# Ten weight chunks leave PSUM before they are split, in a fused attention and feed-forward kernel

## The chip, the cores and the metric

The kernel runs on one core of a Trainium2 chip. The time is the device time of one execution in microseconds (us), taken as the median of several runs. The engines are TensorE (PE: matmuls, PEld its weight loads), VectorE (DVE), ScalarE (ACT), GpSimd (POOL) and SyncE (SP, which issues the DMAs here). SBUF is the on-chip memory, PSUM the small one into which TensorE writes.

## What is computed

Windowed attention, then a feed-forward layer with a rational activation, then a gated one. All is float32, over 2304 tokens:

```python
h = x @ w_in                       # x: attention output, 2304 x 512; w_in 512 x 2048
P = a[0] + a[1]*h + a[2]*h*h + a[3]*h*h*h
Q = 1.0 + abs(b[0])*abs(h) + abs(b[1])*h*h
x = (P / (Q + 1e-06)) @ w_out      # w_out 2048 x 512
gate = 1.0 / (1.0 + np.exp(-(x @ w_gate)))          # w_gate, w_val 512 x 1536
out = (gate * (x @ w_val)) @ w_out2
```

## The kernel before

A float32 operand is split into a high part, which TensorE's fast float32 form takes exactly, and a low part, the difference. A product is then three fast matmuls (`mm3`, L741): high by high, high by low, low by high. Tokens are cut into five blocks of up to 512. The phases are (1, block 0), (2, block 0), and then blocks in pairs; phase kind 1 is the rational layer (`step1`, L752), kind 2 the gated one (`step2`). A step treats one weight chunk of 128 features. In the first phase there are 16 steps: `hidden` (12 matmuls into a bank of pool "h"), the activation, and `product` (matmuls on L841, whole float32 in this phase alone).

The activation of a step is a chain over three engines: on ScalarE the cubic (L775), the abs (L771), the slope (L780), the logarithm (L798) and its exponential (L801), `rest` (L815); on GpSimd `quad` (L789) and `correct` (L820); on VectorE two `horner` (L792), `check` (L804) and `ratio` (L823). A step takes up to four temporaries of pool "t" (11 tiles in SBUF) for it; the one of the cubic is held until `product` has read it.

Weights come in float64, as pairs of 32-bit words, and `weights` (L406) makes float32 of each chunk at its first use: a load on SyncE (L420), `rescale` (L429), `sign` (L442, GpSimd), `shift` (L445, VectorE), `low_bits` (L450, VectorE), then `hi` (a copy, L320 on ScalarE, L322 on VectorE, L324 on GpSimd) and `lo` (a subtraction, L327 on VectorE or GpSimd). A store (L404) follows for chunks that are used again. The intermediate lies in a tile of pool "t" (`wt`) for the first eight chunks and for those of the second layer. For the other chunks of w_in and w_out in the first phase (`banked`) it lies in PSUM, in one of the two buffers of pool "a" (`wb`). GpSimd doesn't read PSUM in this kernel, so for `banked` chunks only ScalarE does `hi` and only VectorE does `lo`. Chunks of w_out are kept `whole` in the first phase and have neither.

Who does what, and in which order, is set by a list planner (`Plan`, L59) at build time. An operation has a priority (its due time), one or more ways (an engine and a cost each), and slots that it takes and uses. An operation that can go to several engines goes where its estimated end is best. A slot is free again when all that use it are planned to be done; an operation that can't get one of a pool holds back those behind it that take from the same pool. Ways marked PORT (VectorE instructions whose operands lie in SBUF, and all of GpSimd's) are planned one at a time over both engines; `dvep` marks a way without that. Each engine then runs its instructions in the planned order.

Of the kernel before, what the change touches and what calls it, by code (L numbers as in the profile page):

```python
# [7 lines left out]
F32 = mybir.dt.float32  # L8
F32R = mybir.dt.float32r
BF16 = mybir.dt.bfloat16  # L10
U32 = mybir.dt.uint32
# [49 lines left out]
class Plan:  # L61
# [14 lines left out]
    def op(self, prio, ways, fn, deps=(), takes=(), uses=(), after=None, table=None):  # L76


        o = Op(prio, ways, fn, deps, takes, uses, after, table)
        for s in o.uses:  # L80
            s.left += 1
        for d in o.deps:
            d.next.append(o)
        if after:
            after.then.append(o)
        self.ops.append(o)
        return o
# [133 lines left out]
def act(n, psum=False, ptrs=0):  # L221
    return ("ACT", n / 1200 + (0.05 if psum else 0.093) + 0.093 * ptrs)


def dve(n, ptrs=0):

    return ("DVE", n / 960 + 0.15 + 0.03 * ptrs, *PORT)


def dvep(n, ptrs=0):  # L230

    return ("DVE", n / 960 + 0.14 + 0.03 * ptrs)


def dve2(n, ptrs=0):
    return ("DVE", n / 1920 + 0.15 + 0.03 * ptrs, *PORT)


def pool(n):
    return ("POOL", n / 477 + 0.17, *PORT)  # L240


def pool1(n, ptrs=0):
    return ("POOL", n / 960 + 0.07 + 0.03 * ptrs, *PORT)


def dma(nbytes, count=1):
    return ("SP", nbytes / Plan.DMA_RATE, count)
# [3 lines left out]
def tile_window_attention__rational_ffn__glu(  # L252
# [48 lines left out]
    op = plan.op  # L301
# [7 lines left out]
    def tile_of(slot, shape, dt=F32, name=None):  # L309
        return pools[slot.pool].tile(shape, dt, tag=slot.pool, name=name or slot.pool)  # L310
# [4 lines left out]
    def temp(slot, name, dt=F32):  # L315
        return tile_of(slot, [P, 512], dt, name)

    def copy(e, out, in_):
        if e == "ACT":
            nc.scalar.copy(out, in_)  # L320
        elif e == "DVE":
            nc.vector.tensor_copy(out, in_)  # L322
        else:
            nc.gpsimd.tensor_scalar(out=out, in0=in_, scalar1=1.0, scalar2=1.0, op0=ALU.mult, op1=ALU.mult)  # L324

    def lo_part(e, out, in_, hi):
        ENGINES[e].tensor_tensor(out=out, in0=in_, in1=hi.bitcast(F32), op=ALU.subtract)  # L327
# [10 lines left out]
    lnb, two, exb = (biases[:, n:n + 1] for n in range(3))  # L338
# [59 lines left out]
    def place(z, keys):  # L398
        for key in keys:
            chunk[key] = z["hi"], z["lo"]  # L400

    def keep(c, what):
        d = stored[c] = dr.tile(list(what.shape), F32, tag=f"w{c[0]}{c[1]}", name=f"w{c[0]}{c[1]}")
        nc.sync.dma_start(out=d, in_=what)  # L404

    def weights(c, prio, keys, again):  # L406

        n = before.get("n", 0)
        before["n"] = n + 1
        banked = c[0] in "iO" and n >= 8
        whole = c[0] == "O"
        raw_s, t_s, w_s = Slot("w"), Slot("a" if banked else "t"), Slot("w")
        z = {}

        def load(e):
            z["w"] = tile_of(raw_s, [P, 1024], U32, "wraw")
            nc.sync.dma_start(out=z["w"], in_=srcs[c[0]][c[1]].bitcast(U32))  # L420
            z["low"], z["high"] = (z["w"].rearrange("p (f t) -> p f t", t=2)[:, :, n] for n in range(2))

        def rescale(e):
            t = z["t"] = tile_of(t_s, [P, 512], U32, "wb" if banked else "wt")
            w = z["c"] = tile_of(w_s, [P, 2, 512], F32R, "w")
            z["hi"], z["lo"] = w[:, 0, :], w[:, 1, :]
            x = z["high"].bitcast(F32)
            if e == "ACT":
                nc.scalar.activation(out=t.bitcast(F32), in_=x, func=AF.Copy, scale=REBIAS * REBIAS)  # L429
            else:  # L430
                ENGINES[e].tensor_scalar(
                    out=t.bitcast(F32), in0=x, scalar1=REBIAS, scalar2=REBIAS, op0=ALU.mult, op1=ALU.mult
                )

        def sign(e):
            if e == "DVE":
                nc.vector.tensor_scalar(
                    out=z["high"], in0=z["high"], scalar1=0x80000000, scalar2=None, op0=ALU.bitwise_and
                )
            else:  # L440
                x = z["high"].bitcast(F32)
                nc.gpsimd.tensor_scalar(out=x, in0=x, scalar1=0.0, scalar2=0.0, op0=ALU.mult, op1=ALU.mult)  # L442

        def shift(e):
            nc.vector.scalar_tensor_tensor(  # L445
                out=z["t"], in0=z["t"], scalar=3, in1=z["high"], op0=ALU.logical_shift_left, op1=ALU.bitwise_or
            )

        def low_bits(e):
            nc.vector.scalar_tensor_tensor(  # L450
                out=z["hi"].bitcast(U32) if whole else z["t"], in0=z["low"], scalar=29, in1=z["t"],
                op0=ALU.logical_shift_right, op1=ALU.bitwise_or,
            )
            if whole:
                for key in keys:
                    chunk[key] = z["hi"].bitcast(F32)

        def hi(e):
            copy(e, z["hi"], z["t"].bitcast(F32))

        def lo(e):
            lo_part(e, z["lo"], z["t"].bitcast(F32), z["hi"])
            place(z, keys)

        def store(e):
            keep(c, z["hi"].bitcast(F32) if whole else z["c"].bitcast(F32))

        o = before["load"] = op(
            -200.47 + 0.92 * n if n < 8 else prio - 6.66,
            [dma(4096 * P)], load, [*before.get("sizes", [])[-RAWS:][:n >= RAWS]], [raw_s], after=before.get("load")  # L470
        )
        one, two = (dvep(512), [act(512, True)]) if banked else (dve(512), [act(512), dve2(512), pool1(512)])
        o = before["size"] = before["take"] = op(
            prio, two, rescale, [o, before.get("size")], [t_s, w_s], [raw_s],
            before.get("take"),
        )
        before.setdefault("sizes", []).append(o)
        o = op(prio, [pool1(512)] if banked else [pool1(512), dve2(512)], sign, [o], uses=[raw_s])
        o = op(prio, [one], shift, [o], uses=[t_s, raw_s])
        o = op(prio, [one], low_bits, [o], uses=[t_s, raw_s] + [w_s] * whole)  # L480
        if not whole:
            o = op(prio, two, hi, [o], uses=[t_s, w_s])
            o = op(prio, [one] if banked else [pool(512), dve(512)], lo, [o], uses=[t_s, w_s])
        for key in keys:
            chunk_ops[key], chunk_slot[key] = o, w_s
        if again:
            stored[c] = op(prio + 4, [dma((2048 if whole else 4096) * P)], store, [o], uses=[w_s])
# [519 lines left out]
    uses = []  # L1007
# [37 lines left out]
    o = op(-195, [dma(128 * P, 2)], coefficients)  # L1045
# [5 lines left out]
    for n, (c, t, keys) in enumerate(fills):  # L1051
        if c in [x for x, *_ in fills[:n]]:
            reload(c, t - 8, keys)
            continue
        again = c in [x for x, *_ in fills[n + 1:]]
        if c[0] == "o":
            split_up(c, t - 2.83, keys, again)
        else:
            weights(c, t - 2.83, keys, again or c[0] == "O")
# [80 lines left out]
```

## Time and profile before

| | |
|---|---|
| median of 3 runs | 958.06 us (957.92 to 958.8) |
| the profiled execution | 958.63 us, span of its instructions 956.9 us |
| PE busy | 938.5 us (98% of the span) |
| DVE busy | 692.2 us (72%) |
| ACT busy | 475.6 us (50%) |
| POOL busy | 268.5 us (28%) |
| mean granted clock of TensorE | 0.996 of full speed |

The first phase runs up to some 150 us of the span, and in it all engines are near their limit; later TensorE alone is. Shares over the whole span are means over such different stages. A group of the profile stands for one line, engine and operation; a chain of work is followed back from the last instruction to what released each.

### The profile page before, as it was taken

How to read it: one execution, taken by the hardware profiler on the slowest of the kernel's cores; microseconds unless marked ns; L12 is line 12 of the kernel's file. 1: busy time of each engine (PE TensorE's matmuls, PEld its weight loads, DVE VectorE, ACT ScalarE, POOL GpSimd, SP SyncE). 2: the span in 40 equal slices, each digit the busy share in tenths (PEclk: the TensorE clock that was granted, in tenths of full speed). 3: DMA queues.
4: the chain of work that ended last, by engine and by line, in shares of the span. 5: the costliest groups of instructions: out<-in, count | busy, mean ns of one | idle time of the engine just before them, and what ended most of it. 6: DMA issues, size and time to landing. Idle time of an engine off the chain costs nothing.

```text
span 956.9 us, 13938 instructions
## 1 busy us (share of the span) xinstructions
PE 938.5 (98%) x4984; PEld 795.2 (83%) x4984; DVE 692.2 (72%) x1189; ACT 475.6 (50%) x975; POOL 268.5 (28%) x277
## 2 busy tenths in 40 slices
PE   8899989999999999999999999999999999999998
PEld 7755647888898999999999998888888888888886
DVE  6999999999999998977567775988998532222221
ACT  6888875566778576644234435544666310001001
POOL 5576652333355242311111112344312000000000
PEclk9999999999999999999999999999999999999999
DMA  9977898999992058853138873100455520013001
GB/s 272 385 260 248 284 313 299 335 349 324 315 385 88 1 155 259 290 175 110 36 95 285 276 241 128 45 1 23 140 193 196 176 66 23 0 45 110 1 1 44
DMA packets 77476, 166.71 MB, mean 174 GB/s; under 512 B 24992, under 2 KB 34208, under 8 KB 77408
## 3 DMA queue, kind: packets, MB, share of 16 engines
q1 hardware_dynamic: 77408, 165.83, 51.1%
q8 instruction: 39, 0.64, 0.3%
q14 instruction: 29, 0.24, 0.1%
HBM read 121.24 MB, written 44.56 MB: 173 GB/s over the span
## 4 chain that ended last, share of the span: by engine, by line
PE 85%; DVE 9%; ACT 3%; issue 1%; DMA 1%; POOL 0%; SPq 0%; DVEq 0%; POOLq 0%; ACTq 0%
PE h L743 32%; PE y L743 29%; PE a L743 15%; PE y L841 4%; PE a L591 2%; PE a L665 1%; DVE et L656 1%; ACT sm L614 1%; DVE tg L792 1%; DVE w L327 1%; PE a L386 1%; DVE mx L606 1%; DVE wt L445 1%; DVE tq L804 1%; DVE tg L823 0%
## 5 line engine op out<-in xcount | busy, mean ns | idle before, releaser
L743 PE MATMUL h<-x,w 128*128 128x512 f32 (+1 forms) x1680 | 373.8, 371 | 3.4 <-DVE tg L792 1.7
L743 PEld LDWEIGHTS h<-x,w 128*128 128x128 f32 x1680 | 305.7, 188 | 51.2 <-issue 3.8
L743 PE MATMUL y<-g,w 128*128 128x384 f32 (+1 forms) x768 | 163.7, 362 | 0.1
L743 PE MATMUL a<-x,w 128*128 128x512 f32 (+1 forms) x720 | 158.9, 369 | 0.0
L743 PE MATMUL y<-w,g 128*128 128x512 f32 x648 | 158.4, 392 | 0.0
L743 PEld LDWEIGHTS y<-g,w 128*128 128x128 f32 x768 | 138.9, 188 | 15.4 <-DVE g L327 0.3
L933 ACT ACTIVATE sg<-h 128x512 f32<-128x512 f32 (+1 forms) x60 | 33.4, 556 | 235.3 <-PE h L743 235.2
L743 PEld LDWEIGHTS a<-x,w 128*128 128x128 f32 x720 | 130.6, 188 | 16.9
L743 PEld LDWEIGHTS y<-w,g 128*128 128x128 f32 x648 | 120.5, 188 | 24.0
L936 DVE TENSOR_TENSOR sg<-sg,a 128x512 f32<-128x512 f32 (+1 forms) x60 | 37.9, 632 | 116.7 <-PE a L743 116.1
L792 DVE SCALAR_TENSOR_TENSOR tg<-tg,ca_sb,h 128x512 f32<-128x512 f32 (+1 forms) x160 | 109.6, 689 | 17.2 <-ACT ta L771 13.9
L789 POOL TENSOR_TENSOR tq<-tq,ta 128x512 f32<-128x512 f32 (+1 forms) x63 | 84.0, 1334 | 83.8 <-ACT tq L780 72.0
L798 ACT ACTIVATE tr<-tq,biases 128x512 f32<-128x512 f32 (+1 forms) x80 | 54.4, 680 | 73.0 <-POOL tq L789 60.6
L823 DVE SCALAR_TENSOR_TENSOR tg<-tg,ca_sb,tr 128x512 f32<-128x512 f32 (+1 forms) x80 | 67.8, 849 | 1.3 <-POOL tr L820 1.2
L775 ACT ACTIVATE tg<-h,ca_sb 128x512 f32<-128x512 f32 (+1 forms) x80 | 51.4, 643 | 34.0 <-PE h L743 33.2
L804 DVE SCALAR_TENSOR_TENSOR tq<-tq,tr 128x512 f32<-128x512 f32 (+1 forms) x80 | 54.6, 682 | 12.3 <-ACT tr L801 10.1
L841 PE MATMUL y<-tg,w 128*128 128x512 f32 x128 | 59.2, 609 | 2.8 <-DVE tg L823 2.8
L442 POOL TENSOR_SCALAR wraw<-wraw 128x512 f32<-128x512 f32 x55 | 45.3, 831 | 59.0 <-ACT wt L429 41.3
L656 DVE STREAM_TRANSPOSE et<-sm 32x256 f32<-32x256 f32 x128 | 55.8, 436 | 2.2
L784 POOL TENSOR_SCALAR tq<-ta,cb_sb 128x512 f32<-128x512 f32 (+1 forms) x34 | 26.7, 786 | 107.1 <-ACT ta L771 105.2
L801 ACT ACTIVATE tr<-tr,biases 128x512 f32<-128x512 f32 (+1 forms) x80 | 54.3, 679 | 1.7
L322 DVE CAST g<-sg 128x512 fp32r<-128x512 f32 (+1 forms) x31 | 15.2, 490 | 48.6 <-PE y L743 48.5
(106 smaller groups left out, 1050.6 us busy)
## 6 DMA issues: line engine op xcount, KB each, us to landing
w<-wp SPq DMA_DIRECT2D x30, 512.0 KB, 3.4
wraw<-in_moe_w_out_dram SPq DMA_DIRECT2D x28, 512.0 KB, 5.7
w<-wv SPq DMA_DIRECT2D x26, 512.0 KB, 3.5
w<-wg SPq DMA_DIRECT2D x25, 512.0 KB, 3.3
w<-wo SPq DMA_DIRECT2D x19, 512.0 KB, 4.2
vv<-in_v_dram SPq DMA_DIRECT2D x35, 256.0 KB, 4.7
wraw<-in_moe_w_in_dram SPq DMA_DIRECT2D x16, 512.0 KB, 8.0
wi<-w SPq DMA_DIRECT2D x16, 512.0 KB, 3.2
```

What stands on the lines that cost most here:

```text
L442: nc.gpsimd.tensor_scalar(out=x, in0=x, scalar1=0.0, scalar2=0.0, op0=ALU.mult, op1=ALU.mult)
L656: nc.vector.transpose(out=to[cols, :, rows], in_=at[rows, :, cols])
L743: nc.tensor.matmul(p, lhs(a), rhs(b), start=first and n == 0, stop=last and n == 2)
L775: nc.scalar.activation(out=z["g"], in_=z["h"], func=AF.Copy, scale=ca_sb[:, 3:4])
L789: ENGINES[e].tensor_tensor(out=z["q"], in0=z["q"], in1=z["a"], op=ALU.mult)
L792: return lambda e: nc.vector.scalar_tensor_tensor(out=z["g"], in0=z["g"], scalar=ca_sb[:, m:m + 1], in1=z["h"], op0=ALU.add, op1=ALU.mult)
L798: nc.scalar.activation(out=z["r"], in_=z["q"], func=AF.Ln, scale=LN_SCALE, bias=lnb)
L801: nc.scalar.activation(out=z["r"], in_=z["r"], func=AF.Exp, scale=-1.0, bias=exb)
L804: nc.vector.scalar_tensor_tensor(out=z["q"], in0=z["q"], scalar=1.0 + 1e-6, in1=z["r"], op0=ALU.add, op1=ALU.mult)
L823: nc.vector.scalar_tensor_tensor(out=z["g"], in0=z["g"], scalar=ca_sb[:, 0:1], in1=z["r"], op0=ALU.add, op1=ALU.mult)
L841: nc.tensor.matmul(yacc[b][m][:, :n], w[:, m * P:(m + 1) * P], z["g"], start=f == first_f, stop=f == last_f)
L936: nc.vector.tensor_tensor(out=z["t"], in0=z["t"], in1=z["v"], op=ALU.mult)
```

## The change

In `weights`, chunks that are `banked` and not `whole` (ten chunks of w_in) take one more tile, from pool "t", at `low_bits`, which writes its result there (`wa`) instead of back into PSUM. `hi` and `lo` read that tile. With that, both may go to other engines: `hi` to ScalarE, VectorE or GpSimd, `lo` to GpSimd or VectorE, by the ways that the chunks in SBUF have had. The PSUM buffer is used up to `low_bits`, no longer up to `lo`. For the other chunks `hi` and `lo` keep their ways.

```diff
         raw_s, t_s, w_s = Slot("w"), Slot("a" if banked else "t"), Slot("w")
+
+        a_s = Slot("t") if banked and not whole else t_s
...
         def low_bits(e):
+            z["all"] = temp(a_s, "wa", U32) if banked and not whole else z["t"]
             nc.vector.scalar_tensor_tensor(
-                out=z["hi"].bitcast(U32) if whole else z["t"], in0=z["low"], scalar=29, in1=z["t"],
+                out=z["hi"].bitcast(U32) if whole else z["all"], in0=z["low"], scalar=29, in1=z["t"],
...
-            copy(e, z["hi"], z["t"].bitcast(F32))
+            copy(e, z["hi"], z["all"].bitcast(F32))
...
-            lo_part(e, z["lo"], z["t"].bitcast(F32), z["hi"])
+            lo_part(e, z["lo"], z["all"].bitcast(F32), z["hi"])
...
-        o = op(prio, [one], low_bits, [o], uses=[t_s, raw_s] + [w_s] * whole)
+        o = op(prio, [one], low_bits, [o], [a_s] * (a_s is not t_s), [t_s, raw_s] + [w_s] * whole)
         if not whole:
-            o = op(prio, two, hi, [o], uses=[t_s, w_s])
-            o = op(prio, [one] if banked else [pool(512), dve(512)], lo, [o], uses=[t_s, w_s])
+            o = op(prio, [act(512), dve2(512), pool1(512)], hi, [o], uses=[a_s, w_s])
+            o = op(prio, [pool(512), dve(512)], lo, [o], uses=[a_s, w_s])
```

## Rows read from the trace of the kernel before

**Rows 1.** Busy us by stretch: from:to, length, engines (instructions), TensorE clock, DMA share, GB/s.

```profile
33.50:69.40 35.90, 32.28 (x109) 20.21 (x108) 34.41 (x51) 28.52 (x48) 24.45 (x22) 0.95 0.81 304
69.40:118.90 49.50, 49.50 (x161) 30.33 (x162) 45.51 (x71) 42.55 (x70) 31.79 (x32) 1.00 0.78 268
118.90:153.10 34.20, 28.30 (x99) 16.12 (x97) 31.31 (x51) 23.31 (x56) 18.66 (x17) 0.95 0.88 302
153.10:956.90 803.80, 797.80 (x4305) 700.57 (x4305) 556.97 (x962) 358.21 (x721) 174.79 (x175) 1.00 0.45 152
```

**Rows 2.** Pieces of the chain that ended last: start us, length us, what.

```profile
79.24 2.73 PE h L743 x12
...
118.97 3.43 PE y L841 x8
122.41 2.73 PE h L743 x12
...
153.07 2.77 PE h L743 x11
```

**Rows 3.** TensorE's groups, 33.5 to 69.4: count, busy us, mean ns, idle before.

```profile
L743 PE MATMUL h<-x,w 128*128 128x512 f32 x84 | 21.3, 404 | 0.5 <-DVE tg L792 0.2 <-DVE w L327 0.2
L841 PE MATMUL y<-tg,w 128*128 128x512 f32 x24 | 12.5, 678 | 2.2 <-DVE tg L823 2.2
```

**Rows 4.** Instructions on tile wb: ns min/median/max, first and last start us.

```profile
L450 DVE SCALAR_TENSOR_TENSOR w<-wraw,wb x14: 673/680/689, 45.4 to 142.9; 128x512 uint32<-128x512 uint32 x14
L450 DVE SCALAR_TENSOR_TENSOR wb<-wraw,wb x10: 680/686/695, 49.8 to 116.3; 128x512 uint32<-128x512 uint32 x10
L320 ACT CAST w<-wb x10: 564/582/591, 50.5 to 117.1; 128x512 fp32r<-128x512 f32 x10
L327 DVE TENSOR_TENSOR w<-wb,w x10: 677/682/692, 55.1 to 118.2; 128x512 fp32r<-128x512 f32 x10
```

**Rows 5.** Copies and subtractions from wt, tile w and line 327.

```profile
L320 ACT CAST w<-wt x33: 600/621/630, 32.4 to 263.2; 128x512 fp32r<-128x512 f32 x33
L327 DVE TENSOR_TENSOR w<-wt,w x31: 672/684/1699, 29.4 to 253.9; 128x512 fp32r<-128x512 f32 x31
L327 POOL TENSOR_TENSOR w<-wt,w x11: 1267/1291/1623, 59.7 to 265.3; 128x512 fp32r<-128x512 f32 x11
```

**Rows 6.** The shift, line 445, from SBUF (wt) and from PSUM (wb).

```profile
L445 DVE SCALAR_TENSOR_TENSOR wt<-wt,wraw x44: 676/684/1772, 25.4 to 258.7; 128x512 uint32<-128x512 uint32 x44
L445 DVE SCALAR_TENSOR_TENSOR wb<-wb,wraw x24: 683/692/710, 44.2 to 142.1; 128x512 uint32<-128x512 uint32 x24
```

**Rows 7.** Chain at 68.00; timelines of TensorE and VectorE (start, length, [idle before <-releaser]).

```profile
68.00 0.60 DVE w L327
...
69.40 2.97 PE L743 MATMUL h<-x,w 128*128 128x512 f32 x12 [0.96 <-DVE tg L792]
...
118.19 0.68 DVE L327 TENSOR_TENSOR w<-wb,w 128x512 fp32r<-128x512 f32 x1
118.80 0.90 DVE L823 SCALAR_TENSOR_TENSOR tg<-tg,ca_sb,tr 128x512 f32<-128x512 f32 x1
```

**Rows 8.** VectorE's groups of `ratio` and `check`, 69.4 to 118.9.

```profile
L823 DVE SCALAR_TENSOR_TENSOR tg<-tg,ca_sb,tr 128x512 f32<-128x512 f32 x10 | 8.3, 837 | 0.0
L804 DVE SCALAR_TENSOR_TENSOR tq<-tq,tr 128x512 f32<-128x512 f32 x8 | 5.6, 701 | 2.8 <-POOL wraw L442 1.6 <-ACT tr L801 1.1
```

**Rows 9.** ScalarE's timeline at four places.

```profile
45.24 0.69 ACT L775 ACTIVATE tg<-h,ca_sb 128x512 f32<-128x512 f32 x1 [0.22 <-PE h L743]
...
52.76 0.58 ACT L771 ACTIVATE ta<-h 128x512 f32<-128x512 f32 x1
...
55.85 0.64 ACT L429 ACTIVATE wb<-wraw 128x512 f32<-128x512 f32 x1 [1.04 <-DVE w L327]
...
128.67 0.72 ACT L798 ACTIVATE tr<-tq,biases 128x512 f32<-128x512 f32 x1 [2.81 <-PE y L841]
```

**Rows 10.** SyncE's timeline: the last store of a w_in chunk.

```profile
122.54 0.33 SPq L404 DMA_DIRECT2D wi<-w  x1
```

## Prediction of the time after the change

> **What bounds the kernel now.** I read the busy times by stretch first [rows 1]. TensorE is busy for 32.3 + 49.5 + 28.3 + 797.8 = 907.9 of 923.4 us, or 98%, so a gain must come out of the few places where it waits. A busy TensorE is not yet one at its pace, so I next priced its work from two steady pieces of the chain [rows 2]: the 12 matmuls of one `hidden` take 2.73 us, the 8 records of one `product` of the first phase 3.43 us; one step of that phase is 6.16 us.
>
> - From 33.5 to 69.4 there are 84 records of `hidden` and 24 of `product` [rows 3]: 84 x 2.73/12 + 24 x 3.43/8 = 29.4 us of work in 35.9 us. TensorE loses 6.5 us there, with VectorE busy for 34.4 of the 35.9 [rows 1].
> - From 69.4 to 118.9 TensorE is busy throughout [rows 1], piece after piece. What speeds other engines can't show here at once.
> - From 118.9 to 153.1 it idles for 34.2 - 28.3 = 5.9 us, and VectorE is busy for 31.3 [rows 1]: the last chains of the first phase, attention units and the chunks of the second phase meet. The second phase starts at 153.07 [rows 2].
> - After that TensorE is busy for 797.8 of 803.8 us [rows 1]; what is won or lost before is carried to the end.
>
> So some 12 us lie in two places where VectorE and what feeds it set the pace. The ten edited chunks are worked on between 49.8 and 118.9 [rows 4]: they touch the end of the first place and lead up to the second.
>
> **The change, part by part.** It concerns w_in chunks 6 to 15: ten `low_bits` from PSUM to PSUM, ten `hi` and ten `lo` [rows 4]. No instruction and no DMA is added or removed.
>
> *`low_bits` with an SBUF output.* The same line writes SBUF for w_out chunks: 680 ns against 686 [rows 4]. Nothing.
>
> *`hi` from SBUF.* On ScalarE 621 ns from SBUF [rows 5] against 582 from PSUM [rows 4]: 10 x 0.04 = 0.4 us on an engine that is idle for 7 of 49.5 us [rows 1]. Nothing; without that cover 0.4 us.
>
> *`lo`, the point of the edit.* On VectorE it takes 682 ns [rows 4], 0.60 us from start to start (68.00 to the end of its piece [rows 7]); on GpSimd 1291 ns [rows 5]. The planner has had this choice for chunks that lie in SBUF and gave 11 of 42 to GpSimd [rows 5]. I take 3 of 10: VectorE gets 3 x 0.6 = 1.8 us back (bounds 0 and 6.0), GpSimd 3 x 1.29 = 3.9 us more.
>
> *The price of an SBUF operand.* The line that shifts has a longest time of 1772 ns over 44 instructions with both inputs in SBUF, and of 710 ns over 24 with one in PSUM, at nearly the same median [rows 6]. I read this as VectorE's two-SBUF-input instructions standing still while GpSimd works. Every edited `lo`, now free of this, joins the shared time, on whichever engine. From 69.4 to 118.9 it is already taken for 31.8 us by GpSimd [rows 1] and by 10 `ratio` and 8 `check` of VectorE [rows 8], 18 x 0.61 = 11.0 us (0.61 is `lo` to `ratio`, start to start [rows 7]): 42.8 of 49.5 us, 86%. Seven `lo` on VectorE make it 47.0 (95%), seven on GpSimd 51.8 (105%). Delayed by it are `quad`, `correct`, `check` and `ratio` of the steps. In this stretch they have cover: `ratio` of step 12 starts at 118.80 [rows 7], its `product` at 122.41 + 2.73 = 125.14 [rows 2]. Without the cover, before 69.4 and after 118.9, a `lo` costs between 0 and 1.29 us; I take 0.3, near the low end, since only two or three `lo` lie there.
>
> The Trainium skill speaks against the change at this point. "Perfetto Trace Analysis", Optimizing Scalar/DVE Operations, says that moving work between VectorE and GpSimd might not help, since they share an SBUF read port; "SBUF — State Buffer", Who interferes with whom, that a VectorE instruction with two SBUF inputs contends with a GpSimd instruction that reads SBUF. The maxima of [rows 6] agree. By that rule the relief of 1.8 us would be given back; what comes of it at worst is the second rival.
>
> *VectorE's relief where it counts at once.* In the chain the `lo` of chunk 8 (68.00, 0.60 us) lies before the last `horner` for which `hidden` of step 7 waits; TensorE had stood for 0.96 us [rows 7]. On GpSimd it leaves 0.6 us; kept on VectorE, nothing. Bounds 0 and 0.96; I take 0.3.
>
> *The PSUM buffer.* Pool "a" has two buffers. A chunk held its own from `rescale` to `lo`, now only to `low_bits`; a `rescale` on ScalarE waited 1.04 us for such a `lo` [rows 9]. These chunks run at (118.19 - 68.00)/7 = 7.2 us each [rows 7], the steps at (122.41 - 79.24)/7 = 6.2 us [rows 2], so chunks fall back: 10.6 us ahead of their use for chunk 8 (68.6 against 79.24), 3.6 for chunk 15 (118.8 against 122.41). Freed earlier, they can run ahead into VectorE's 4.0 idle us between 69.4 and 118.9 [rows 1], and the gate and value chunks behind them start earlier, before the crowded stretch. Bounds 0 and 4.0 us (all of that idle time filled). I take 0.9, near the low end, because of the next row.
>
> *The tile of pool "t", a new wait.* `low_bits` now needs one of 11 temporaries, of which a step holds up to four. They are short twice: the abs at 52.76 belongs to the step whose cubic ran at 45.24, and at 128.67 a logarithm, which takes a new tile, waited 2.81 us for a `product` that frees one [rows 9]. A `wa` holds a tile from `low_bits` to `lo`; while `low_bits` waits for one, VectorE's queue behind it stands (the next shift, `horner`, `check`), and ScalarE waits for `horner` and `check`. Chunk 6 falls into the first shortage; chunk 15 is gone before the second. Bounds 0 and 2.81 us; I take 0.3, nearer to none, since the ten tiles are held one at a time. Stores come after `lo` in SyncE's queue, ahead of later weight loads; the last is issued at 122.54, 3.7 us after its `lo` ended at 118.87 [rows 7, 10], so a `lo` later by 0.6 us is covered there.
>
> *The sum.* Against the profiled execution of 958.63 us (span 956.9, 1.73 outside it; 0.57 above the median): -0.3 - 0.9 + 0.3 + 0.3 = -0.6, so 958.0. Against the median: 958.06 - 0.6 = 957.5 us. That is no change by what can be measured here (0.2%, 1.9 us).
>
> **The rivals.** *Faster: the chunks run ahead.* For it: buffers refilled as soon as they are free, the falling lead, and 5.9 idle us at the second place. Against it: tiles are short there. Price: three quarters of the 4.0 us, 3.0, to 955.0; all of it and half of the 0.6 before step 7, 953.8.
>
> *Slower: the shared time is full.* It decides from the point where the planner gives more than four of the seven steady `lo` to GpSimd (42.8 + 4 x 1.29 + 3 x 0.6 = 49.8 against 49.5). Then `correct` and `ratio` fall back, and from 118.9 on, where a chain no longer has 6 us of cover, every us reaches TensorE. Price: 51.8 - 49.5 = 2.3 us, to 960.4; with what the two early ones cost (0.3), 960.7. For it: the 86%. Against it: the planner's 11 of 42.
>
> *Slower by the tile.* `wa` of chunk 6 takes the tile for which the abs at 52.76 waits, and that chain moves by 2.8 us less the 0.6 won: 958.06 + 2.2 = 960.3.
>
> *Nothing moves off VectorE.* The planner may keep all ten `lo` there; only buffer and tile change then, and the time stays in the forecast's own case.
>
> **How the numbers follow.** No measurable change 0.40; the chunks run ahead 0.35; shared time full 0.18; the tile 0.07. One changed choice lets the planner order everything behind it anew, so no case is sharp. The range goes from the end of the first rival, 953.8, to that of the second, 960.7. The forecast's own case reaches from 956.2 to 959.9.
>
> **What would show it.** `lo`: about three GpSimd instructions that read `wa`; those on VectorE with a longest time well over 692 ns [rows 4]. Buffer: `rescale` no longer waits for a `lo`. Run-ahead: the last w_in `lo` before 117, VectorE idle for under 3 us up to 118.9, the second phase's first matmul before 152. The prediction is wrong if that matmul (153.07 [rows 2]) comes over 2 us earlier or later, or if the time after it changes by more than 1 us.

## The result, and the profile after

The changed kernel takes 972.54 us (median of 4 runs, 971.76 to 972.98) against 957.99 us of the kernel before on the same chip: the ratio is 1.0143 [1.0131, 1.0154], 13.7 us slower by the ratio, 14.6 by the medians. Forecast were 957.5 us and a range of 953.8 to 960.7. The profiled execution took 971.76 us with a span of 969.2, that is 12.3 more span than before. All medians here are of undisturbed executions; one of e3 below, 1342 us at a granted clock of 0.654, is left out of its median. In the changed kernel the lines behind the edit have numbers higher by 2 or 3 (L743 is L746, L450 is L453).

First the stretches of [rows 1], read from the changed kernel (same columns):

```profile
33.50:69.40 35.90, 32.14 (x108) 20.51 (x109) 33.08 (x47) 28.30 (x46) 22.66 (x20) 0.95 0.70 266
69.40:118.90 49.50, 49.50 (x159) 29.71 (x159) 47.09 (x68) 41.57 (x68) 35.34 (x35) 1.00 0.81 289
118.90:153.10 34.20, 28.97 (x102) 16.03 (x101) 32.25 (x53) 24.32 (x52) 20.99 (x21) 0.95 0.92 329
153.10:956.90 803.80, 793.74 (x4270) 696.82 (x4269) 554.80 (x964) 363.14 (x726) 172.47 (x172) 0.99 0.45 150
```

Up to 153.1 TensorE is as busy as before to within 0.7 us in each of them. GpSimd has 3.6 us more between 69.4 and 118.9, and VectorE, which should have been relieved, 1.6 us more.

Next the instructions on the new tile (ns min/median/max, first and last start), which answer to [rows 4, 5]:

```profile
L453 DVE SCALAR_TENSOR_TENSOR wa<-wraw,wb x10: 673/677/689, 55.1 to 119.3; 128x512 uint32<-128x512 uint32 x10
L320 ACT CAST w<-wa x8: 601/606/622, 55.9 to 113.9; 128x512 fp32r<-128x512 f32 x8
L327 DVE TENSOR_TENSOR w<-wa,w x6: 677/768/1674, 60.0 to 114.7; 128x512 fp32r<-128x512 f32 x6
L327 POOL TENSOR_TENSOR w<-wa,w x4: 1279/1290/1301, 82.2 to 122.1; 128x512 fp32r<-128x512 f32 x4
```

Four `lo` and two `hi` (L324, 617 ns in the median) went to GpSimd; the `lo` on VectorE have a longest time of 1674 ns where it was 692. The first `low_bits` comes at 55.1 instead of 49.8, and the last `lo` at 122.1 instead of 118.2.

Then TensorE's waits from 150 us on (what waited, for whom; us in total, times, longest), the kernel before first, the changed one second. All of them:

```profile
PE h L743 <- DVE x L327: 1.4, 1, 1.4
PE a L665 <- ACT et L320: 1.0, 1, 1.0
PE h L743 <- DVE tg L792: 0.5, 1, 0.5
PE a L665 <- DVE et L656: 0.3, 1, 0.3
```

```profile
PE a L746 <- ACT sm L617: 4.1, 1, 4.1
PE a L642 <- DVE sm L631: 3.3, 1, 3.3
PE h L746 <- DVE tg L795: 0.9, 1, 0.9
PE y L746 <- DVE g L327: 0.8, 2, 0.6
PE a L668 <- DVE et L659: 0.6, 1, 0.6
PE a L592 <- ACT et L320: 0.3, 1, 0.3
PE y L746 <- POOL g L324: 0.2, 1, 0.2
```

The two largest are new, and neither names a w_in chunk. The loss has two parts. A marker that both kernels have is the sigmoid of the gated layer, step by step: one at 198.03 before is at 204.48 after (6.45 later), the one at 226.21 at 232.66 (6.45), and the one at 479.76 at 492.10 (12.34). So some 6.4 us are lost by 198, nothing up to 226, 5.9 between 226 and 480, and nothing more from there to the end (span 12.3).

The first loss, at the start of the second phase. TensorE before:

```profile
146.10 1.54 PE L591 MATMUL a<-kt,q_diag 128*128 128x128 f32 x8
147.47 3.60 PE L841 MATMUL y<-tg,w 128*128 128x512 f32 x8
...
153.07 2.77 PE L743 MATMUL h<-x,w 128*128 128x512 f32 x11 [1.35 <-DVE x L327]
155.68 2.88 PE L743 MATMUL a<-x,w 128*128 128x512 f32 x12
158.40 2.88 PE L743 MATMUL h<-x,w 128*128 128x512 f32 x12
```

and after:

```profile
150.85 0.94 PE L746 MATMUL h<-x,w 128*128 128x512 f32 x3
...
152.30 1.05 PE L594 MATMUL a<-kt,q_diag 128*128 128x128 f32 x8
153.11 2.32 PE L746 MATMUL h<-x,w 128*128 128x512 f32 x9
159.54 5.42 PE L746 MATMUL a<-x,w 128*128 128x512 f32 x12 [4.11 <-ACT sm L617]
164.80 2.92 PE L746 MATMUL h<-x,w 128*128 128x512 f32 x12
```

The gate product (L746 into `h`) is in time, 153.11 against 153.07. The value product that follows needs a bank of pool "a". Before, the scores of the attention unit (L591) were computed ahead of the last `product` of the first phase, at 146.10; now their second half stands inside the first gate product, at 152.30, and both banks are held until ScalarE has taken their exponentials (L617; their sum is read behind each). ScalarE in that time:

```profile
155.04 0.36 ACT L617 ACTIVATE sm<-a,mx 128x128 f32<-128x128 f32 x1
...
155.49 1.28 ACT L1084 ACT_TABLE_LOAD   x1
156.79 0.60 ACT L936 ACTIVATE sg<-h 128x512 f32<-128x512 f32 x1
157.39 1.28 ACT L1084 ACT_TABLE_LOAD   x1
158.68 0.37 ACT L617 ACTIVATE sm<-a,mx 128x128 f32<-128x128 f32 x1
```

In the middle of the exponentials stands the first sigmoid, with a table load of 1.28 us on either side: 1.28 + 0.60 + 1.28 = 3.16 us in which a bank stays taken. When TensorE resumes, it is at the lower of its two clock levels, 1.2 of 2.4 GHz (columns as in [rows 1]; the granted clock is the third number from the end, 0.51):

```profile
159.50:164.90 5.40, 5.36 (x13) 4.22 (x14) 2.56 (x6) 1.96 (x9) 0.00 (x0) 0.51 0.98 395
```

The twelve matmuls take 5.42 us instead of 2.88. Wait and clock together: 4.11 + 5.42 - 2.88 = 6.65 us, and the next gate product is 164.80 - 158.40 = 6.40 late.

### The profile page after: what moved, and what is told of

The parts are those of the page before. It is cut to its first block, busy times and chain, and to the rows that moved or that the text cites. A ratio compares the mean times of both kernels' runs of the same rounds, so it can differ in the third digit from the quotient of the medians.

```text
span 969.2 us, 13906 instructions
## 1 busy us (share of the span) xinstructions
PE 942.7 (97%) x4984; PEld 797.0 (82%) x4984; DVE 693.3 (72%) x1190; ACT 481.5 (50%) x977; POOL 270.2 (28%) x278
## 4 chain that ended last, share of the span: by engine, by line
PE 65%; DVE 6%; ACT 3%; issue 1%; DMA 1%; POOL 1%; SPq 0%; POOLq 0%; DVEq 0%; ACTq 0%
PE y L746 26%; PE h L746 25%; PE a L746 11%; PE a L594 1%; DVE et L659 1%; ACT sm L617 1%; PE a L668 1%; DVE wt L447 1%; DVE w L327 1%; DMA w<-wO 1%; POOL w L327 0%; ACT w L320 0%; ACT L1084 0%; DVE tg L795 0%; DVE tq L792 0%
## 5 line engine op out<-in xcount | busy, mean ns | idle before, releaser
L746 PE MATMUL h<-x,w 128*128 128x512 f32 (+1 forms) x1680 | 376.5, 373 | 2.3 <-DVE tg L795 1.8
L746 PEld LDWEIGHTS h<-x,w 128*128 128x128 f32 x1680 | 306.7, 188 | 50.2 <-issue 5.6
L746 PE MATMUL a<-x,w 128*128 128x512 f32 (+1 forms) x720 | 161.5, 373 | 4.1 <-ACT sm L617 4.1
L746 PE MATMUL y<-g,w 128*128 128x384 f32 (+1 forms) x768 | 164.5, 363 | 0.9 <-DVE g L327 0.8
L746 PE MATMUL y<-w,g 128*128 128x512 f32 x648 | 158.5, 392 | 0.0
L746 PEld LDWEIGHTS y<-g,w 128*128 128x128 f32 x768 | 139.7, 189 | 16.7 <-DVE g L327 1.3
L746 PEld LDWEIGHTS a<-x,w 128*128 128x128 f32 x720 | 132.1, 190 | 21.9 <-ACT sm L617 4.5
L746 PEld LDWEIGHTS y<-w,g 128*128 128x128 f32 x648 | 120.5, 188 | 24.0
L826 DVE SCALAR_TENSOR_TENSOR tg<-tg,ca_sb,tr 128x512 f32<-128x512 f32 (+1 forms) x80 | 72.8, 910 | 0.2
L844 PE MATMUL y<-tg,w 128*128 128x512 f32 x128 | 61.4, 626 | 4.8 <-DVE tg L826 4.8
L844 PEld LDWEIGHTS y<-tg,w 128*128 128x128 f32 x128 | 24.9, 198 | 33.2 <-issue 25.5
L327 DVE TENSOR_TENSOR g<-sg,g 128x512 fp32r<-128x512 f32 (+1 forms) x51 | 35.1, 688 | 20.1 <-POOL g L324 18.5
```

The costliest lines, as they stand in the source:

```text
L746: nc.tensor.matmul(p, lhs(a), rhs(b), start=first and n == 0, stop=last and n == 2)
L826: nc.vector.scalar_tensor_tensor(out=z["g"], in0=z["g"], scalar=ca_sb[:, 0:1], in1=z["r"], op0=ALU.add, op1=ALU.mult)
L844: nc.tensor.matmul(yacc[b][m][:, :n], w[:, m * P:(m + 1) * P], z["g"], start=f == first_f, stop=f == last_f)
```

## The experiments

Two theories stood against each other. *The order*: what the edited instructions cost by themselves is small; the edit made the planner order everything anew, and the new order has conflicts elsewhere, which another small cause would have brought as well. *The edit*: its own work (shared time, tile, GpSimd) costs the 14 us. All ratios are to the kernel before on the same chip.

### The edit in the order of before

**e1** writes `low_bits` to SBUF and leaves plan, engines and order as they were; the tile is taken from pool "g", which is little used in the first phase.

```diff
-                out=z["hi"].bitcast(U32) if whole else z["t"], in0=z["low"], scalar=29, in1=z["t"],
+                out=z["hi"].bitcast(U32) if whole else z.setdefault("all", temp(Slot("g"), "wa", U32) if banked else z["t"]), ...
...
-            copy(e, z["hi"], z["t"].bitcast(F32))
+            copy(e, z["hi"], z["all"].bitcast(F32))
...
-            lo_part(e, z["lo"], z["t"].bitcast(F32), z["hi"])
+            lo_part(e, z["lo"], z["all"].bitcast(F32), z["hi"])
```

> The edit's operands with the old order: every engine's list of operations is that of the kernel before, but the ten low_bits write an SBUF tile (of pool g, which is idle in the first phase), and hi and lo read it; hi stays on ScalarE, lo on VectorE. Order theory (the 14.5 us come from the new order that the planner made, not from the edited instructions): 957 to 959 us. Shared-time theory (two SBUF inputs make lo stand still beside GpSimd, up to 1.7 us instead of 0.68 for one): ten lo at up to 1.0 more, 960 to 968 us. Tile theory (the loss is the wait for a temporary of pool t): 957 to 959, since none is taken.

**e2** is e1 with all ten `lo` on GpSimd, at their old places in the order.

```diff
-            lo_part(e, z["lo"], z["all"].bitcast(F32), z["hi"])
+            lo_part("POOL" if banked else e, z["lo"], z["all"].bitcast(F32), z["hi"])
```

> As the same-order kernel, but all ten lo run on GpSimd, each at its old place in the order. Order theory: 956 to 961 us. Shared-time theory: ten times 1.29 us more of shared time between the two engines, in a stretch that is 86% taken, so 963 us and more.

**e12** is e1 with four of them there, as many as the changed kernel has.

```diff
-            lo_part(e, z["lo"], z["all"].bitcast(F32), z["hi"])
+            lo_part("POOL" if banked and c[1] in (10, 12, 13, 15) else e, z["lo"], z["all"].bitcast(F32), z["hi"])
```

> The order of before, with low_bits written to SBUF and four of the ten lo on GpSimd (w_in chunks 10, 12, 13 and 15), as many as the changed kernel has there; the other six stay on VectorE. It is the local content of the edit without a new order. Theory (the order decides): within 3 us of the kernel before, between the runs with none (959.7) and with ten (960.6) on GpSimd or just below them, 958 to 961 us. Rival (this mix of engines costs the time by itself): 963 us or more.

| `lo` on GpSimd | median us | ratio | by the ratio |
|---|---|---|---|
| none (e1) | 959.71 | 1.0017 [1.0005, 1.0030] | +1.6 us |
| four (e12) | 959.73 | 1.0009 [1.0000, 1.0018] | +0.9 us |
| ten (e2) | 960.61 | 1.0027 [1.0016, 1.0037] | +2.6 us |

The local content of the edit, without the tile of pool "t" and without the two `hi` on GpSimd, costs 1 to 3 us, whoever does `lo`, and not 14. e1 lies between what the order theory (up to 959) and the theory of the shared time (from 960) had expected. The `lo` in e1 (ns min/median/max), then in e12:

```profile
L327 DVE TENSOR_TENSOR w<-wa,w x10: 678/1164/1774, 54.4 to 119.9; 128x512 fp32r<-128x512 f32 x10
```

```profile
L327 DVE TENSOR_TENSOR w<-wa,w x6: 683/1204/1768, 57.1 to 115.2; 128x512 fp32r<-128x512 f32 x6
L327 POOL TENSOR_TENSOR w<-wa,w x4: 1288/1302/1710, 89.0 to 123.2; 128x512 fp32r<-128x512 f32 x4
```

At the same places in the order, with the same engine, an SBUF operand alone takes the median from 682 ns [rows 4] to 1164. The ten on VectorE add up as follows (count | busy us, mean ns), before and in e1:

```profile
L327 DVE TENSOR_TENSOR w<-wb,w 128x512 fp32r<-128x512 f32 x10 | 6.8, 682 | 0.0
```

```profile
L327 DVE TENSOR_TENSOR w<-wa,w 128x512 fp32r<-128x512 f32 x10 | 12.2, 1222 | 0.0
```

That is 5.4 us more of VectorE's time. The trace of e1 also shows when a `lo` is stretched: the one at 106.75, with no GpSimd instruction beside it, took 0.68 us, and the two that ran wholly beside `quad` and `correct` (54.43 and 78.03) took 1.77 each. Only a small part of it reaches the end: the two sigmoids at 198.03 and 479.76 are at 198.84 and 480.55 in e1, so it loses 0.8 us by 198 and nothing from there.

### The order disturbed without the edit, and with it

Three numbers by which the planner estimates durations are altered by 0.3% to 4%, each once in the kernel before and once in the changed one. No computation changes, only what the planner makes of it.

```diff
-    DMA_FIXED, DMA_RATE = 2.0, 361e3
+    DMA_FIXED, DMA_RATE = 2.0, 360e3
```

> The kernel before, with the planner's estimate of the DMA rate at 360e3 in place of 361e3 (0.3%). No instruction changes, only the order in which they are listed. Order theory: the time moves by more than 2 us although nothing of the edit is there, upward, to 960 to 972, if the order before was a favourable one. The other theories: 957 to 959 us.

> The changed kernel with the same alteration of the planner's estimate (360e3). Order theory: it leaves 972.5 us by more than 2 us, most likely downward, to 960 to 970. The other theories: 971 to 974 us, since the edited instructions are all there.

```diff
-    return ("DVE", n / 960 + 0.14 + 0.03 * ptrs)
+    return ("DVE", n / 960 + 0.145 + 0.03 * ptrs)
```

> The kernel before with another small alteration of an estimate: a VectorE operation with an operand in PSUM is planned with 0.145 in place of 0.14 us of fixed cost. Order theory: over 2 us away from 958, upward (960 to 970). Others: 957 to 960.

> The changed kernel with that same alteration. Order theory: anywhere from 960 to 974 us, without a fixed distance to the kernel before under the same alteration. Others: 971 to 974.

```diff
-    return ("POOL", n / 477 + 0.17, *PORT)
+    return ("POOL", n / 474 + 0.17, *PORT)
```

> The kernel before with GpSimd's two-input operations planned 0.6% longer. Order theory: away from 958 by 2 us or more, most likely upward, 960 to 968. Others: 957 to 960.

> The changed kernel with GpSimd's cost rate 474 in place of 477, the same alteration that took the kernel before to 962.6 us. Theory (the order decides): a third time that follows no rule of the edit, somewhere between 960 and 973 us; together with the other two altered pairs (966.1 against 963.6, 964.1 against 966.7) the mean of the three with the edit lies within 3 us of the mean of the three without it, 964.3. Rival (the edit itself costs its 14 us): every order with the edit is slow, the mean of the three stays 5 us or more above 964.3, and this run is above 970.

| altered | kernel before | changed kernel |
|---|---|---|
| nothing | 957.99 | 972.54, 1.0143 [1.0131, 1.0154] |
| DMA rate | 966.05, 1.0076 [1.0059, 1.0093] (e3) | 963.60, 1.0058 [1.0043, 1.0074] (e4) |
| VectorE's fixed cost | 964.09, 1.0060 [1.0045, 1.0075] (e6) | 966.71, 1.0091 [1.0076, 1.0107] (e7) |
| GpSimd's rate | 962.64, 1.0050 [1.0033, 1.0066] (e8) | 964.12, 1.0047 [1.0032, 1.0063] (e9) |
| mean of the three | 964.26 | 964.81 |

Without the edit each alteration costs 4.7 to 7.5 us; with the edit each one gains 5.8 to 8.9. These are differences of medians; by the ratios the gains are 5.0 to 9.2. The means differ by 0.55 us, where single orders differ by 3 us on either side and the pairs by -2.5 to +2.6. So the kernel before has an unusually good order, the changed kernel an unusually bad one, and between ordinary orders three pairs show no difference that could be told from their scatter. That excludes a fixed cost of 14 us; a cost or gain of a few us by the edit itself it doesn't exclude. e3 is given by its times alone.

The altered kernels e6 and e8 show the same wait as the changed one, with no edit in them. TensorE in e6 and in e8 (start, length, what, [idle before <-releaser]):

```profile
160.38 4.62 PE L743 MATMUL a<-x,w 128*128 128x512 f32 x12 [3.49 <-ACT sm L614]
```

```profile
157.19 4.60 PE L743 MATMUL a<-x,w 128*128 128x512 f32 x12 [4.10 <-ACT sm L614]
```

The first value product waits for the exponentials for 3.5 and 4.1 us and then runs slowly, 4.6 us. In e8 the first sigmoid stands between these exponentials with its two table loads, as in the changed kernel; in e6 it stands ahead of all of them. In e4, e7 and e9, which have the edit, the value product starts with no such wait, but the gate product before it ends 5.0, 4.5 and 3.2 us later than in the kernel before (160.79, 160.30 and 159.06 against 155.84): these orders lose those us in the first phase. Another order thus also loses its time at another place, and whether the edit has a share in the lateness of these three is open.

### One conflict undone by hand

**e5** is the changed kernel with one instruction moved after planning: the first sigmoid goes behind the exponentials of the attention unit that it interrupted. Nothing else moves.

```diff
         ops = plan.order()
+        first_gate = next(n for n, o in enumerate(ops) if o.fn.__name__ == "gate")
+        end = max(n for n, o in enumerate(ops[:first_gate + 60]) if o.table == LN_EXP and o.start < ops[first_gate].start + 6)
+        ops.insert(end, ops.pop(first_gate))
```

> The changed kernel with one operation moved in the order after planning: the first sigmoid of the second phase comes behind the exponentials of the attention unit that is being worked on, instead of between them. In the changed kernel two table loads of 1.28 us and the sigmoid stand between those exponentials; they hold a PSUM buffer of pool a, for which the first value product waits 4.11 us. Local theory (this is the first half of the loss): that wait falls below 1.5 us and the time to 967 to 970 us. If the wait only shows a delay that has its cause elsewhere: 971 to 974 us.

966.24 us, ratio 1.0085 [1.0070, 1.0100]: 6.3 us less than the changed kernel by the medians, 5.6 by the ratios (967 to 970 was expected), by one instruction that has nothing to do with w_in (with it, one of the two table loads falls away at that place). TensorE there:

```profile
153.13 2.32 PE L746 MATMUL h<-x,w 128*128 128x512 f32 x9
156.25 3.03 PE L746 MATMUL a<-x,w 128*128 128x512 f32 x12 [0.80 <-ACT sm L617]
159.12 2.88 PE L746 MATMUL h<-x,w 128*128 128x512 f32 x12
```

The wait falls from 4.11 to 0.80 us, the twelve matmuls run in 3.03 us, and the next gate product starts at 159.12 instead of 164.80. The first loss is hereby shown. The second is still there: the sigmoid at 479.76 before is at 486.35 here, where the one at 198.03 is at 198.75 (0.7 late instead of 6.4), so 5.9 us are lost between them as in the changed kernel.

The second loss I can only read. From the sigmoid at 226.21 to that at 479.76 in the kernel before, and between the same two in the changed one (columns as in [rows 1]):

```profile
226.21:479.76 253.55, 251.53 (x1559) 238.85 (x1558) 216.98 (x393) 154.43 (x338) 82.08 (x85) 1.00 0.56 189
232.66:492.10 259.44, 253.61 (x1559) 240.43 (x1558) 217.81 (x394) 158.74 (x340) 78.95 (x81) 0.99 0.54 183
```

With the same number of matmul records TensorE idles for 5.83 us instead of 2.02 and is busy for 253.61 instead of 251.53: 3.81 + 2.08 = 5.89 us, the whole of this loss. The largest wait is here (TensorE, then ScalarE):

```profile
287.06 2.25 PE L746 MATMUL h<-x,w 128*128 128x384 f32 x12
292.62 0.63 PE L642 MATMUL a<-ident,sm 128*128 128x128 f32 x4 [3.32 <-DVE sm L631]
293.37 3.01 PE L746 MATMUL h<-x,w 128*128 128x384 f32 x11
```

```profile
290.88 0.60 ACT L801 ACTIVATE tr<-tq,biases 128x384 f32<-128x384 f32 x1
291.38 0.56 ACT L778 ACTIVATE tg<-h,ca_sb 128x384 f32<-128x384 f32 x1
...
292.84 0.85 ACT L774 ACTIVATE ta<-h 128x384 f32<-128x384 f32 x2
```

Transposes of an attention unit (L642) wait 3.32 us for the division of its exponentials by their sum (L631). As after the first wait, TensorE is slow behind it; the granted clock is 0.58 here:

```profile
293.90:298.00 4.10, 4.10 (x16) 4.10 (x15) 3.34 (x7) 3.25 (x7) 1.39 (x2) 0.58 0.67 270
```

By this clock some 1.7 of the 2.08 us are lost in these 4.1 us (an estimate: 4.1 x 0.42). The `hidden` behind the transposes starts at 293.37, just after the first of the two abs (L774, 292.84), which reads a bank of pool "h" and stands on ScalarE behind the unit's exponentials, a logarithm and a cubic. Moving the transposes alone would then have gained little. No run undoes this wait: where the 5.9 us lie is read from the trace, that the order of these instructions is their cause is argued, not shown.

### The edit's parts, each with a new order

**e10** takes the extra tile from pool "g" instead of "t".

```diff
-        a_s = Slot("t") if banked and not whole else t_s
+        a_s = Slot("g") if banked and not whole else t_s
```

> The changed kernel with the extra tile from pool g, which is little used in the first phase, in place of pool t: no low_bits waits for a tile of pool t. Rival (the tile): chunk 6's low_bits is back at about 50 us and the time falls to 960 or below. Theory (the order decides): low_bits is back at about 50 us too, but the time is another draw, 960 to 970 us, since the planner orders the rest anew; a loss at another place shows in the waits of TensorE.

967.18 us, 1.0079 [1.0058, 1.0101]. Its `low_bits` and the `lo` on GpSimd:

```profile
L453 DVE SCALAR_TENSOR_TENSOR wa<-wraw,wb x10: 670/678/689, 49.4 to 118.9; 128x512 uint32<-128x512 uint32 x10
...
L327 POOL TENSOR_TENSOR w<-wa,w x4: 1278/1352/1715, 57.9 to 121.5; 128x512 fp32r<-128x512 f32 x4
```

Chunk 6's `low_bits` is back at 49.4: it was the tile of pool "t" for which the planner held it until 55.1. The time is still 7.6 us above the kernel before by the ratio, so those 5 us of delay are not what costs the 14 us. The largest wait after 150 us is now another one, of a `hidden` for an abs:

```profile
PE h L746 <- ACT ta L774: 3.1, 1, 3.1
```

**e11** keeps `hi` on ScalarE and `lo` on VectorE for the ten chunks; buffer and tile are as in the change.

```diff
-            o = op(prio, [act(512), dve2(512), pool1(512)], hi, [o], uses=[a_s, w_s])
-            o = op(prio, [pool(512), dve(512)], lo, [o], uses=[a_s, w_s])
+            o = op(prio, [act(512)] if banked else [act(512), dve2(512), pool1(512)], hi, [o], uses=[a_s, w_s])
+            o = op(prio, [dve(512)] if banked else [pool(512), dve(512)], lo, [o], uses=[a_s, w_s])
```

> The changed kernel with hi kept on ScalarE and lo on VectorE for the ten chunks: only the buffer that is freed earlier and the extra tile remain, with an order planned anew. Rival (GpSimd's work and the shared time): the time falls back to that of the kernel before, 957 to 960 us. Theory (the order decides): it does not fall back for that reason; some us are lost after 153 us at an attention unit or at a step whose buffers are held, 960 to 970 us.

965.35 us, 1.0059 [1.0035, 1.0082]: with nothing on GpSimd the time does not come back either. Its ten `lo`:

```profile
L327 DVE TENSOR_TENSOR w<-wa,w x10: 678/688/1129, 59.3 to 122.0; 128x512 fp32r<-128x512 f32 x10
```

They have the operands and the engine of e1, but a median of 688 ns instead of 1164: here the planner, which counts them as PORT, has made the order for them. So the stretch of e1 belongs to an order that wasn't made for these operands. Here too a `hidden` waits 3.1 us for an abs, at 288.92, and the value product does not wait for the exponentials. Either alteration of the edit gives another ordinary order, 6 to 8 us above before, and neither part can be named as the cause.

## Why the prediction was wrong, point by point

- **What bounds the kernel.** TensorE, with few places of idle time: right. But I looked for what the edit could do to the two places before 153 and took the rest as carried to the end unchanged. The loss lies in the part that I held fixed: up to the second phase's first gate product both kernels need the same time (153.11 against 153.07 [rows 2]; these are its later matmuls, the first ran at 150.85 against 151.22), and the 12.3 us come after it. The second of the two conditions that I gave for being wrong is met, the first is not.
- **`low_bits`, `hi`**: 677 ns and 606 on ScalarE where I had 680 and 621; two `hi` went to GpSimd, which the sum had left out. No part of the result.
- **`lo`**: four on GpSimd where I took three. The relief of VectorE did not come: its busy time in the steady stretch rose by 1.6 us instead of falling by 1.8.
- **The shared time.** The mechanism was right, and in an unchanged order its price was read too low. I allowed 0.3 us; e1, e12 and e2 measure 0.9 to 2.6 for the whole of the local terms there, where relief and price had been set at 0.3 each. For a new order, as in e11, the runs don't give the price apart. "Perfetto Trace Analysis" of the Trainium skill, Optimizing Scalar/DVE Operations, says that a move between VectorE and GpSimd might not help, because of a shared SBUF read port. The runs agree: none, four or ten `lo` moved in the old order gave 1.0017, 1.0009 and 1.0027. By that rule one would have expected about no gain, not a loss of 14 us. The second rival's end, 960.7, is close to where e2 ended (960.61), but hardly by its mechanism: that has the loss reach TensorE from 118.9 on, and in e2's trace the steps have fallen behind by 82 (the cubic of step 4 starts 0.74 us later than in the kernel before, that of step 8 3.90, that of step 15 4.24). Its 86% was low, too: it took 0.61 us for each `ratio` and `check`, a distance measured behind a `lo`, where [rows 8] has them busy for 8.3 + 5.6 = 13.9 us, up to 92% in all.
- **The PSUM buffer.** No `rescale` waits for a `lo` any more (ScalarE's only waits of that kind are 1.1 us for a `low_bits` of w_out). But the chunks did not run ahead, which was the largest term (-0.9) and the likelier of the two large rivals: the last `lo` came at 122.1, later than before, and `hidden` of step 15 waited for it, by 0.2 us. In e10, where no tile of pool "t" is needed, the last `lo` is at 121.5 all the same: in these orders neither the buffer nor the tile set the pace of the chunks.
- **The tile of pool "t".** Named for chunk 6, and there it was: 5.3 us late. Its price on the end was close to nothing in this order, since the start of the second phase did not move.
- **The failed step** is the sum, which has local terms alone and none for the new order. The prediction names that term, "One changed choice lets the planner order everything behind it anew, so no case is sharp", but puts it at nothing, without a reason, and lets the range end at the sum of local bounds. The runs showed in its place: three alterations that do nothing else cost 4.7 to 7.5 us in the kernel before, and the changed kernel's own new order loses 6.4 and 5.9 us at two places behind 153. With that term the middle would have been about 964, the changed kernel's 972.5 still an unlucky draw, and "slower" the likely side.
- Could it have been read from the trace of before? In part. The scores of the attention unit stand just ahead of the last `product`, and the waits of TensorE listed above come to 3.2 us in the 800 us after the first phase: an order that good, in a kernel whose TensorE is busy for 98% of the span, has little room to improve and much to lose when it is drawn again. How much could only be measured.

## What to carry to other kernels

Where a planner sets the order, an edit has two prices: what its instructions cost in the old order, and what the new order costs. Measure them apart, the first with the order held, the second by altering a planner's estimate that nothing depends on; when the second scatters by more than the first, a sum of local terms says little of the result, and a comparison of one order with one order little of the edit. And when an edit loses time far behind its place, look for the instruction that a few us of reordering put between others, as this sigmoid among exponentials: moving it gave back about as much here (5.6 us by the ratios in e5) as a part of the edit altered, with its new order (6.1 in e10, 8.0 in e11).

## What the runs showed of the hardware

- An operand moved from PSUM to SBUF made the same VectorE subtraction, at the same place in the order, 1164 ns in the median and up to 1774 instead of 682 and 692 (e1), and 688 and 1129 in an order planned for it (e11). `low_bits`, which has its second input in PSUM and writes SBUF, stayed between 666 and 691 ns on the new tile in all runs that have it. GpSimd's `lo` is stretched too, but less often: 1.30 us in the median, 1.71 at most (e12).
- One sigmoid of 0.60 us among exponentials costs ScalarE 3.16 us, because of a table load of 1.28 us on either side. "ScalarE: Activation LUTs" of the Trainium skill, What ACT_TABLE_LOAD costs, gives 1283 ns for the load, which agrees, and a drain of about 1380 ns besides for each switch. The trace shows none: the load follows the last exponential's reading (155.29 + 0.20) at 155.49, and the sigmoid starts at 156.79, 0.02 us after the load's end.
- A wait of TensorE can cost more than its length: after 4.1 us of standing still its granted clock was 0.51 of full speed, the lower level, and the next twelve matmuls took 5.42 us instead of 2.88. Behind the wait of 0.8 us in e5 they took 3.03, at a granted clock of 1.00.
